# Input transfers of a fused three-layer kernel: fewer issued by ScalarE, full rows, and a work order planned anew

## The chip, the cores and the metric

The kernel runs on one core of a Trainium2 chip. The metric is the device time of one execution in microseconds (us). Engines: TensorE (PE, with PEld for its weight loads), VectorE (DVE), ScalarE (ACT), GpSimd (POOL) and SyncE (SP). DMA transfers are issued by SyncE or by ScalarE, each in the order of its own instructions ("SPq" and "ACTq" in the rows), and are carried out by 16 DMA engines.

## The reference

Three layers follow each other, for 4 batches of 576 tokens and 512 channels, all in 32-bit floats.

```python
# 1: attention, 8 heads of 64; 4 heads "local", 4 "strided"
mask_local   = (rel >= 0) & (rel < 32)
mask_strided = (rel >= 0) & (pos[None, :] % 32 == pos[:, None] % 32)
x = softmax(where(mask, q @ k.T / 8, -1e9)) @ v
# 2: feed-forward with the token before mixed in
xk = mu_k * x + (1 - mu_k) * x_prev ;  xr = mu_r * x + (1 - mu_r) * x_prev
x = sigmoid(xr @ w_r) * (relu(xk @ w_k) ** 2 @ w_v)      # w_r 512x512, w_k 512x1024, w_v 1024x512
# 3: four experts, each a causal attention of one head of 64; the two best by a gate are summed
out = sum over the token's two experts e of  weight_e * (softmax(q_e k_e.T / 8, causal) @ v_e @ wo_e)
```

The weights of layer 2 come as 64-bit floats, 10.5 MB in all.

## The kernel before

**Recording, planning, issuing.** The kernel does not call the engines in the order in which the work is written. A `Recorder` takes each operation as an `Op`, with what it needs, which buffers it opens and what it costs on each engine that could do it (`price`, L306). The operations are grouped in units with short names, and the string `PLAN` (L23) lists the names in an order that gives each operation its rank. `order` (L389) then plays the program through: for every engine it keeps the time at which it is free, finds the operations whose needs are met, and of those that could start within 0.1 us of the earliest takes the one of lowest rank. An operation whose buffer isn't free isn't a candidate (`begin`, L419). Operations that several engines can do (copies out of PSUM, casts) get their engine here. Where TensorE would stand idle in the first 80 us of that play, products on a tile of zeros are put in to keep it busy (`warm`, L378). The program is then issued in the planned order (`give`, L492 in every row), and each engine runs its own instructions in that order. So a changed cost or a changed string moves instructions everywhere, and no operation is added or lost by it but those warm-up products.

**How the planner times a transfer before.** A transfer issued by SyncE or ScalarE costs the issuer 0.45 us. Before the ninth issue *of one engine* it waits for the landing of that engine's eighth last (L423). The transfer then runs at 0.42 MB per us in the first 8 us and at 0.37 later, on one link, after 1.25 or 2.0 us (L465 to L468), and is counted as landed 0.5 us after that.

**Stage 1 of batch 0** is the head of the program. `pair(hp)` handles two heads: hp 0 and 1 are local, hp 2 and 3 strided. One tile `qkv` of a pair holds queries, keys and values, side by side; there are two such buffers for the local heads, and hp 2 and 3 of batch 0 live in buffers that other tiles use later. Its loads are the units `0L{hp}q` (`load`, L766), `0L{hp}v` (`load_rest`, L810) and `0L{hp}m` (`load_more`, L818). For the local pairs `q` brings the columns of the first two thirds of the tokens, `v` the values of those, `m` the rest; queries are issued by SyncE and keys, values, the local mask and the strided masks by ScalarE. `part` (L762) takes 96 rows (`LK`) for the columns of local values, which have content in 96 of 128 rows, and 128 for everything else. `0S` units hold the scores and the softmax of a third (local) or a group (strided), `0T` the transposes, `0V` the product with the values (tile `pol` or `pos`) that ends in `xT`. A softmax step is: scores on TensorE (`sl`, `ss`), minimum with the mask on VectorE, exponential on ScalarE (`el`, `es`), sum, reciprocal and product on VectorE. The transposes use the tile `ident`, loaded by unit `0i` (L1293).

**Weights.** `weight_pieces` (L620 and on) loads 20 pieces of 512 KB as tile `wraw`: 0 to 3 are w_r, 4 to 7 and 8 to 11 the two halves of w_k, 12 to 19 w_v. Unit `0L{j}` with a plain number is the load, `0W{j}` turns a piece into 32-bit floats (one ScalarE and two VectorE operations), `0P{j}` splits it into a high and a low part. All of them are issued by SyncE.

**Stage 2.** `0Ar`, `0Ak` mix the tokens of the first chunk (320 tokens), `0Ag` are its gate products with w_r (tile `pr`), `0Am` and `0Av` its products with w_k and w_v (tiles `pk`, `pv`); `0Z` are the same for the second chunk (256 tokens). Batches 1 to 3 follow with `1`, `2`, `3` in place of the leading 0; a load of a local pair of a later batch (`1L0`) is nine issues. Stage 3 has small letters.

The lines that order the loads of one local pair in batch 0, before:

```python
w, two = src.shape[1], nc.scalar
z = c + 6 * 2 * D if local else w

def part(a, z, q=nc.sync):
    rows = LK if local and a >= c else P
    q.dma_start(home()[:rows, a:z], src[:rows, a:z])
```

Of the kernel before, what the change touches and what calls it, by code (L numbers as in the profile page):

```python
# [22 lines left out]
PLAN = """  # L23
0L1q 0z 0L0q 0S3 1L1 0L1 wl3 1L0 0S0 0i 0T3 0L2q 0L2v 0L1v 0L3q 0S4 0T4 0V4 0L0v 0T0 0V0 0L3v 0S1 0S6 0L0m 0W1 0T1 0V1 0L15
0V3 0Ar0 0S7 0L0 0W0 0L1m 0L8 1z 0Ak0 0L3 0Ar1 0T7 0L11 0T6 0S9 0L2 0S8 0L6 0S2 0L13 0W2 0V7 0L7 0W7 0S5 0W3 ws30 0V6 0Ar2
0Ak2 0Ak1 0T9 0V9 0T8 0L12 0V8 0L4 0Ar3 0W6 0T5 wl0 ws00 0L5 0W5 0W4 0Ak3 0T2 0V2 0Zr0 0L10 0W10 0V5 0Zr1 0L18 0W18 1L2 0Ag0
0Ag1 0Zr2 0Zr3 0L14 0L9 0W13 1L3 0W9 2L2 0W11 0Am2 0Am3 0L17 0L16 ws31 0W8 0Zk0 ws01 0Am0 0W15 0W14 2L0 0Am1 0P5 2z 0Zk3 0P14
0Ag2 0Zg1 0L19 0W19 1S1 0W12 1S0 0Am4 0Am6 0Am7 0P18 0P6 wl2 2L1 0P19 0P13 0P12 0P15 0Zg3 0Zg0 0Av6 0W16 0P16 0Age 0P4 0Am5
0W17 0Av4 0Av0 0P17 0Zg2 0sig 0Av1 0Zk1 0P1 0P0 2L3 1S3 1S4 0Av5 0P8 1V1 1V4 0Av2 3L0 1S6 1T6 1S8 0Zk2 1V6 1Ar0 1Ak0 1Ar1
0Av3 1Zr0 3L1 1Ar2 1Ak1 0P3 0P7 0Zm2 0Zm3 0Zm0 0P10 3L2 0Av7 0x0 0P11 0P9 0Zm1 0Zm4 1Ak2 0u 0Zm5 0Zm6 0Zm7 0Zv4 0P2 1T8 0Zv6  # L30
0Zv2 0Zv0 1V8 1Ar3 1Ak3 0Zv1 1Am6 0Zv3 2S6 2T6 2V6 1Ag2 2S1 wl1 ws20 2S0 1Am4 2S4 2S3 1Ag0 2V1 2S8 1Ag3 1Zr2 1Ag1 3z 0Zv5
1Am5 1Zr1 1Am7 3L3 1Zr3 1Zg1 1Zg0 1Zk0 1Zk1 1Am2 1Am3 2V4 1Am0 1Am1 2T8 1Zk2 1Zk3 1Zm6 2Ar0 2Ar1 1Zm2 1Av0 0Zv7 1Zg2 2V8 2Ar3
1Zm7 1Zg3 1Av1 1Av4 1Av5 3S1 1Av2 3S0 1Av3 2Ar2 2Ag2 2Ag1 3V1 3S3 1Av6 1Av7 2Ag3 2Ak0 2Ak1 3S4 3V4 1Zm3 2Ag0 1Zm0 1Zm1 1Zv6
1Zm4 1Zm5 1Zv4 1Zv0 2Ak3 2Ak2 2Am0 2Am1 2Am2 2Am3 2Zr0 1Zv2 2Am6 2Am4 2Av4 2Zr1 2Zr2 2Am5 2Zk0 2Am7 1Zv3 1Zv1 2Zr3 1Zv5 2Zg2
2Zk1 2Zg0 3S6 2Zk2 2Zg1 ws10 2Zk3 2Zm4 2Av0 1Zv7 3Ar0 3Ar1 3Ak0 3Zr0 1u 0x1 2Zg3 2Av1 3T6 2Zm2 3V6 2Av6 2Av7 2Av2 2Zm3 2Zm0
2Zm6 2Zm5 3Ar2 3S8 3T8 3V8 1x0 2Zm1 2Zm7 2Zv0 2Zv2 2Zv3 2Zv4 2Zv5 2Av5 3Ar3 3Ag2 3Ak1 3Ak2 2Zv6 3Ag3 ws11 3Ak3 3Am0 3Am2 3Am3
3Zr1 2Zv1 3Am4 2Av3 3Ag1 3Am6 3Zr2 ws21 0v1 3Ag0 3Am5 3Am7 3Am1 3Zr3 3Zg0 3Zg2 3Zk0 3Zg1 3Av2 3Zk2 2Zv7 3Zg3 3Av6 3Av4 2u
3Zk1 3Zk3 3Zm4 3Zm0 3Av0 3Zm1 3Zm2 3Zm3 1x1 3Zm6 3Zm7 3Zm5 mc 3Av1 3Zv4 3u 3Zv0 3Zv6 3Zv2 0v0 0k00 0k01 0q01 0q00 0k10 0v4
0v2 0s0 0k11 1q01 0v3 0g 0m0 0s1 0m1 0p13 1q00 1v1 0q11 0q10 2x0 1k00 0s3 1n 1k01 1v2 0p02 3Av7 0p11 0p01 0s2 0p10 3Zv5 0p03
0t 0p00 0m2 0p22 0m3 0p32 0s40 0s41 0p23 1q10 1q11 1k10 1s1 0p20 0p21 1k11 1v0 0p33 0p12 1s2 0m4 0p41 0p30 0p31 3Zv7 1v3 1g  # L40
1m1 2q00 2k01 0p40 3Av5 1s3 1m3 1p31 0a10 0a11 0a00 0a01 1s0 2k00 0o02 1p32 1m2 3Zv1 0o01 3Zv3 2x1 2q10 1p21 0o03 2k10 1m0
1p12 1p03 1p02 1p10 1p11 1p01 2v2 0o12 1t 0o13 1s40 1s41 2v4 1p20 3n 1m4 3Av3 1p30 2q11 1p22 2t 0o00 2v1 1p41 2q01 0o10 1p23
1p00 2v0 2k11 2s1 1p13 2s40 0o11 1p40 3x0 3q00 2v3 2g 2m1 1p33 2s3 2m3 1a10 1a11 3x1 1a00 1a01 2s2 2m2 1o00 3k01 2p12 2p30
3q10 2p32 2s41 3k10 3q11 3k00 2p22 2p33 2p23 2s0 2m0 2p00 1o12 2m4 3v3 2p40 3v2 2p21 2p20 2p31 2p01 1o01 1o13 2p10 3k11 2p03
2p13 3v0 3v1 2p02 3g 2p11 3t 3s2 3s40 1o03 1o02 3s3 3q01 1o10 3s41 2p41 1o11 3s1 2a00 3m4 2a10 3m2 3p23 2a01 3m3 2a11 3s0
2o13 3p21 3m1 3p22 3p32 3p33 2o00 3p41 3p30 3p40 3m0 3p20 2o11 3p01 3p00 3p11 2o02 3p10 2o03 2o10 3p13 3p02 3p12 3p03 2o01
2o12 3a00 3a01 3p31 3a10 3a11 3o01 3o03 3o13 3o00 3o12 3o11 3o10 3o02
"""
# [1709 lines left out]
```

## Time and profile before

| | us |
|---|---|
| median of 3 runs (lowest, highest) | 509.03 (508.84, 509.15) |
| the profiled execution, its own time | 508.54 |
| its span, first to last instruction | 506.8 |
| TensorE busy in the span | 493.3 |
| VectorE busy | 348.4 |
| ScalarE busy | 280.1 |
| GpSimd busy | 8.6 |

The profile describes one execution. Its span is 1.74 us shorter than the time of the execution. Times in rows count from the span's start. "Busy" is the time in which an engine had an instruction in work; the queues' issuing instructions and waits are not counted. In a timeline a row can hold several like instructions that follow each other, and a wait stands in brackets with what ended it. The DMA share is the mean busy share of the 16 DMA engines.

### The profile page before, as it was taken

The numbers are of one execution on the slowest core, as the hardware profiler recorded it, in microseconds if no ns is written. First come the engines' busy times: TensorE is split into PE (matmuls) and PEld (weight loads), VectorE is DVE, ScalarE is ACT, GpSimd is POOL, SyncE is SP. The second block draws the span as 40 slices with busy tenths as digits, with TensorE's granted clock in tenths as the row PEclk, the third lists the DMA queues.
The fourth block names the chain that finished last, engine by engine and source line by source line (L and its number), as shares of the span: only waits on it lengthen the run. The fifth ranks groups of instructions, "written<-read, shape, count | busy, mean of one in ns | idle before, by whom it ended". The sixth has DMA issues, their size and how long they took to land.

```text
span 506.8 us, 13028 instructions
## 1 busy us (share of the span) xinstructions
PE 493.3 (97%) x5134; PEld 461.2 (91%) x5134; DVE 348.4 (69%) x1206; ACT 280.1 (55%) x831; POOL 8.6 (2%) x43
## 2 busy tenths in 40 slices
PE   4899999999999999999999999999999999999997
PEld 4767789999999999999999999999997998899896
DVE  1699999977858458553596813257999747886950
ACT  1799985646647355344534543124665654466663
POOL 0000000000000000000000000020000000000000
PEclk9599999999999999999999999999999999999999
DMA  8997211423423122000223300042103112001022
GB/s 267 343 396 245 69 63 58 154 61 101 105 69 85 46 83 85 32 1 23 73 64 96 103 27 27 22 117 58 43 1 95 32 38 78 18 27 34 27 95 93
DMA packets 34635, 43.79 MB, mean 86 GB/s; under 512 B 12790, under 2 KB 29006, under 8 KB 34574
## 3 DMA queue, kind: packets, MB, share of 16 engines
q1 hardware_dynamic: 33226, 41.38, 25.9%
q10 hardware_dynamic: 1348, 1.59, 1.0%
q8 instruction: 40, 0.66, 0.5%
q14 instruction: 21, 0.17, 0.1%
HBM read 33.38 MB, written 9.44 MB: 84 GB/s over the span
## 4 chain that ended last, share of the span: by engine, by line
PE 91%; DVE 4%; DMA 2%; ACT 2%; issue 0%; ACTq 0%
PE pk L492 21%; PE pv L492 20%; PE pr L492 10%; PE pvv L492 5%; PE pw L492 5%; PE pq_False L492 5%; PE pq_True L492 5%; PE pt L492 4%; PE s L492 4%; PE py L492 3%; PE ss L492 2%; PE pol L492 2%; PE sl L492 1%; PE ptl L492 1%; PE pos L492 1%; DMA qkv<-in_loc_dram 1%
## 5 line engine op out<-in xcount | busy, mean ns | idle before, releaser
L492 PE MATMUL pv<-kk,wvh 128*128 128x320 f32 (+1 forms) x512 | 103.1, 295 | 0.0
L492 PEld LDWEIGHTS pv<-kk,wvh 128*128 128x128 f32 x512 | 81.5, 188 | 0.5
L492 PE MATMUL pk<-xh,wkh 128*128 128x256 f32 (+1 forms) x224 | 65.7, 293 | 0.0
L492 PE MATMUL pk<-xl,wkh 128*128 128x256 f32 (+1 forms) x224 | 65.4, 292 | 0.0
L492 ACT ACTIVATE rf<-pk 128x320 f32<-128x320 f32 (+1 forms) x64 | 26.2, 410 | 45.0 <-PE pk L492 43.7
L492 ACT ACTIVATE pe<-pe,nm 128x128 f32<-128x128 f32 (+4 forms) x72 | 41.4, 577 | 9.0 <-DVE nm L492 4.7
L492 PEld LDWEIGHTS pk<-xh,wkh 128*128 128x128 f32 x224 | 42.0, 188 | 0.2
L492 PEld LDWEIGHTS pk<-xl,wkh 128*128 128x128 f32 x224 | 42.0, 188 | 0.0
L492 DVE TENSOR_TENSOR sg<-pv,sg 128x320 f32<-128x320 f32 (+1 forms) x32 | 14.6, 455 | 30.2 <-PE pv L492 20.9
L492 DVE CUSTOM_DVE_ANT_0 pe<-s,mcau 128x128 f32<-128x128 f32 (+4 forms) x72 | 32.1, 481 | 0.3 <-PE s L492 0.2
L492 DVE CAST kk<-rf 128x256 fp32r<-128x256 f32 (+1 forms) x41 | 12.6, 307 | 26.9 <-ACT rf L492 18.3
L492 DVE TENSOR_TENSOR kk<-rf,kk 128x320 fp32r<-128x320 f32 (+1 forms) x64 | 28.5, 454 | 2.3 <-ACT kk L492 1.5
L492 PE MATMUL pt<-ident,pe 128*128 128x128 f32 x200 | 30.0, 274 | 0.1
L492 ACT ACTIVATE rf<-rf 128x320 f32<-128x320 f32 (+1 forms) x64 | 28.5, 447 | 1.4
L492 PE MATMUL pr<-xh,wrh 128*128 128x320 f32 (+1 forms) x96 | 28.3, 295 | 0.0
L492 PE MATMUL pr<-xl,wrh 128*128 128x320 f32 (+1 forms) x96 | 28.2, 294 | 0.0
L492 DVE TENSOR_SCALAR pe<-pe,sm 128x384 f32<-128x384 f32 (+4 forms) x72 | 26.0, 400 | 0.2
L492 ACT COPY sg<-pr 128x320 f32<-128x320 f32 (+1 forms) x29 | 11.3, 406 | 26.5 <-PE pr L492 26.5
L492 DVE SCALAR_TENSOR_TENSOR xf<-xd,mu,xT 128x256 f32<-128x256 f32 (+1 forms) x52 | 25.5, 511 | 0.2
L492 ACT COPY aT<-pt 128x512 f32<-128x512 f32 (+3 forms) x52 | 22.5, 454 | 5.5 <-PE pt L492 4.9
L492 ACT ACTIVATE el<-el,nm 128x64 f32<-128x64 f32 (+1 forms) x72 | 24.8, 349 | 0.9 <-DVE nm L492 0.9
L492 PEld LDWEIGHTS pt<-ident,pe 128*128 128x128 f32 x200 | 23.3, 140 | 1.8 <-DVE pe L492 0.6
(309 smaller groups left out, 1445.0 us busy)
## 6 DMA issues: line engine op xcount, KB each, us to landing
wraw<-in_w_v_dram SPq DMA_DIRECT2D x8, 512.0 KB
wraw<-in_w_k_dram SPq DMA_DIRECT2D x8, 512.0 KB
qkv<-in_strd_dram SPq DMA_DIRECT2D x7, 576.0 KB
qkv<-in_loc_dram SPq DMA_DIRECT2D x6, 592.0 KB
x_spill<-sg SPq DMA_DIRECT2D x16, 160.0 KB
...
```

Of the source, the lines that this page charges most:

```text
L492: f[o.engine](*[now(x) for x in a], **{n: now(x) for n, x in k.items()})
```

## The change

It has four parts.

1. ScalarE issues only four transfers: the keys of `0L0q` (two) and `0L1q` (one), and the local mask. The identity (`0i`), the keys of the first strided pair, the values of both local pairs (`0L0v`, `0L1v`) and the two strided masks are issued by SyncE. The keys and queries of the first strided pair become one transfer.
2. Local values are loaded in all 128 rows instead of 96.
3. The planner's model of a transfer is another: its length follows from rows and contiguous runs, with a factor of 1.6 below 126 rows; the wait for the eighth last transfer counts the transfers of both queues together.
4. `PLAN` is another string, found with this model.

```diff
-0L1q 0z 0L0q 0S3 1L1 0L1 wl3 1L0 0S0 0i 0T3 0L2q 0L2v 0L1v 0L3q 0S4 0T4 0V4 0L0v 0T0 0V0 0L3v 0S1 0S6 0L0m 0W1 0T1 0V1 0L15
-0V3 0Ar0 0S7 0L0 0W0 0L1m 0L8 1z 0Ak0 0L3 0Ar1 0T7 0L11 0T6 0S9 0L2 0S8 0L6 0S2 0L13 0W2 0V7 0L7 0W7 0S5 0W3 ws30 0V6 0Ar2
...
+0L1q 0L0q 0S4 0S3 0i 0L3q 0T4 0T3 0L2q 0S1 0T1 0L1v 0S0 0z 0V3 0T0 0S6 1L0 0L1 0L0v 0V1 0V0 0L0m 0S7 0L1m 0S9 0Ar0 0W1 0T7 1u
+0L3 0W3 0V4 0Ar1 0T6 0L0 0W0 0S2 0Ak0 0L2v 0S8 0S5 0V7 0V6 0T9 0Ar2 0L3v 0V9 0L2 0W2 0L5 0L17 1z 0L6 0W6 0T2 0L7 0W5 0T8 0V8
...
@@ price
-            return 0.78 if v.p1 - v.p0 == 54 else 0.45, (v.p1 - v.p0) * v.cols.size * 4 / 1e6, None
+            rows, cols = v.p1 - v.p0, v.cols.reshape(-1)
+            run = int(np.argmax(np.append(np.diff(cols) != 1, True))) + 1
+            t = rows * cols.size / run / 16 * (run * 4 / 27500 + 0.0085) * (1.6 if rows < 126 else 1.0) + 0.07
+            return 0.78 if rows == 54 else 0.45, t, None
@@ order
-        ring = dict.fromkeys(self.ENGINES, 0.0)
-        mode, link, landed, given = None, 0.0, {e: [] for e in self.ENGINES}, []
+        mode, link, landed, given = None, 0.0, [], []
...
-            if o.load and e != "gpsimd" and len(landed[e]) >= 8:
-                s = max(s, landed[e][-8])
+            if o.load and e != "gpsimd" and len(landed) >= 8:
+                s = max(s, landed[-8])
...
-                t = max(ring[e], s + (1.25 if s < 8 else 2.0))
-                link = max(link, t) + o.lag[e] / (0.42 if s < 8 else 0.37)
-                ring[e] = max(link, t + (0.56 if s < 8 else 0.0))
-                o.end = ring[e] + 0.5
-                landed[e].append(o.end)
+                link = max(link, s + 1.5) + o.lag[e]
+                o.end = link + 0.8
+                landed.append(o.end)
@@ pair
             def part(a, z, q=nc.sync):
-                rows = LK if local and a >= c else P
-                q.dma_start(home()[:rows, a:z], src[:rows, a:z])
+                q.dma_start(home()[:, a:z], src[:, a:z])
...
-                    elif hp == 2:
-                        part(0, S)
-                        part(S, c, two)
...
-                    part(c, z, two if local else nc.sync)
+                    part(c, z)
                     if hp == 1:
                         for i, nr in enumerate((7, 6)):
-                            nc.scalar.dma_start(m0[nr], c_str[i, :NN * nr, :NN * nr])
+                            nc.sync.dma_start(m0[nr], c_str[i, :NN * nr, :NN * nr])
...
-    nc.unit("0i", lambda: nc.scalar.dma_start(ident, c_ident))
+    nc.unit("0i", lambda: nc.sync.dma_start(ident, c_ident))
```

## Rows read from the trace of the kernel before

**Rows 1.** The page's first part: busy time, share of the span and instructions by engine.

```profile
PE 493.3 (97%) x5134; PEld 461.2 (91%) x5134; DVE 348.4 (69%) x1206; ACT 280.1 (55%) x831; POOL 8.6 (2%) x43
```

**Rows 2.** Busy time by stretch, the first 30 us; columns in the first line.

```profile
core 0: us, PE busy (x) PEld busy (x) DVE busy (x) ACT busy (x) POOL busy (x), PEclk, DMA share, GB/s
0.00:10.00 10.00, 5.67 (x60) 5.09 (x60) 1.98 (x15) 0.00 (x0) 0.31 (x5) 1.00 0.81 256
10.00:20.00 10.00, 5.39 (x36) 4.74 (x34) 5.47 (x39) 8.05 (x34) 0.00 (x0) 0.53 1.06 317
20.00:30.00 10.00, 9.21 (x113) 7.30 (x112) 7.34 (x39) 7.52 (x34) 0.00 (x0) 0.78 1.03 391
```

**Rows 3.** The same view for the tile of zeros alone, the sum over 0 to 100.

```profile
sum 100.00, PE 4.84 PEld 4.33 DVE 0.17; mean PE 0.48 PEld 0.43 DVE 0.02
```

**Rows 4.** Timeline of ScalarE, 0 to 13.5 us: start, length, engine, instruction, count, [idle before].

```profile
0.73 0.89 ACTq L492 DMA_DIRECT2D qkv<-in_loc_dram  x2
1.65 0.45 ACTq L492 DMA_DIRECT2D mloc<-in_c_loc_dram  x1
2.13 0.45 ACTq L492 DMA_DIRECT2D qkv<-in_loc_dram  x1
3.94 0.33 ACTq L492 DMA_DIRECT2D ident<-in_c_ident_dram  x1
4.79 0.34 ACTq L492 DMA_DIRECT2D qkv<-in_strd_dram  x1
5.74 0.34 ACTq L492 DMA_DIRECT2D qkv<-in_loc_dram  x1
8.05 1.05 ACTq L492 DMA_DIRECT2D mstr<-in_c_str_dram  x2
10.83 0.32 ACTq L492 DMA_DIRECT2D qkv<-in_loc_dram  x1
11.18 1.28 ACT L492 ACT_TABLE_LOAD   x1 [11.18 <-DMA qkv<-in_loc_dram]
12.48 0.37 ACT L492 ACTIVATE el<-el,nm 128x96 f32<-128x96 f32 x1
```

**Rows 5.** Timeline of SyncE's queue, parts of 0 to 53 us.

```profile
0.73 1.33 SPq L492 DMA_DIRECT2D qkv<-in_loc_dram  x3
2.11 0.43 SPq L492 DMA_DIRECT2D wraw<-in_w_r_dram  x1
...
14.10 0.43 SPq L492 DMA_DIRECT2D wraw<-in_w_r_dram  x1
...
42.92 9.97 SPq L492 DMA_DIRECT2D qkv<-in_loc_dram  x17
```

**Rows 6.** Timeline of VectorE, parts of 5 to 14 us.

```profile
5.86 0.26 DVE L492 CUSTOM_DVE_ANT_0 el<-sl,mloc 128x96 f32<-128x96 f32 x1 [4.86 <-DMA mloc<-in_c_loc_dram]
...
13.69 0.17 DVE L492 TENSOR_SCALAR sm<-sm 128x3 f32<-128x3 f32 x1 [5.95 <-ACT el L492]
```

**Rows 7.** Timeline of TensorE, parts of 0 to 32.5 us.

```profile
14.74 0.84 PE L492 MATMUL ptl<-ident,el 128*96 128x128 f32 x3 [4.61 <-ACT el L492]
...
23.12 0.91 PE L492 MATMUL pol<-aTl,qkv 96*64 96x64 f32 x12
...
31.79 0.81 PE L492 MATMUL pr<-xw,w('r', 0)_378 128*128 128x320 f32 x2
```

**Rows 8.** Busy time by stretch, four others; columns as in rows 2.

```profile
12.48:31.79 19.31, 16.19 (x167) 13.35 (x167) 14.60 (x88) 16.08 (x73) 0.01 (x1) 0.69 1.04 367
31.79:100.00 68.21, 67.96 (x802) 56.63 (x803) 66.94 (x211) 57.16 (x169) 0.79 (x5) 1.00 0.44 142
450.00:506.80 56.80, 53.48 (x459) 47.59 (x457) 32.65 (x132) 32.97 (x97) 0.15 (x1) 0.99 0.18 61
...
14.00:16.00 2.00, 1.26 (x7) 0.93 (x9) 1.96 (x18) 2.00 (x11) 0.00 (x0) 0.50 1.10 268
```

**Rows 9.** Waits of SyncE's queue, 0 to 60 us: total, times, longest.

```profile
SPq L492 <- PE pol L492: 6.7, 1, 6.7
```

More of the change, by code (lines that the diff above doesn't have):

```diff
@@ L23 @@
 PLAN = """
-0L1q 0z 0L0q 0S3 1L1 0L1 wl3 1L0 0S0 0i 0T3 0L2q 0L2v 0L1v 0L3q 0S4 0T4 0V4 0L0v 0T0 0V0 0L3v 0S1 0S6 0L0m 0W1 0T1 0V1 0L15
-0V3 0Ar0 0S7 0L0 0W0 0L1m 0L8 1z 0Ak0 0L3 0Ar1 0T7 0L11 0T6 0S9 0L2 0S8 0L6 0S2 0L13 0W2 0V7 0L7 0W7 0S5 0W3 ws30 0V6 0Ar2
-0Ak2 0Ak1 0T9 0V9 0T8 0L12 0V8 0L4 0Ar3 0W6 0T5 wl0 ws00 0L5 0W5 0W4 0Ak3 0T2 0V2 0Zr0 0L10 0W10 0V5 0Zr1 0L18 0W18 1L2 0Ag0
-0Ag1 0Zr2 0Zr3 0L14 0L9 0W13 1L3 0W9 2L2 0W11 0Am2 0Am3 0L17 0L16 ws31 0W8 0Zk0 ws01 0Am0 0W15 0W14 2L0 0Am1 0P5 2z 0Zk3 0P14
@@ L28 @@
[L28 to L46, printed above, removed]
@@ L47 @@
-2o12 3a00 3a01 3p31 3a10 3a11 3o01 3o03 3o13 3o00 3o12 3o11 3o10 3o02
+0L1q 0L0q 0S4 0S3 0i 0L3q 0T4 0T3 0L2q 0S1 0T1 0L1v 0S0 0z 0V3 0T0 0S6 1L0 0L1 0L0v 0V1 0V0 0L0m 0S7 0L1m 0S9 0Ar0 0W1 0T7 1u
+0L3 0W3 0V4 0Ar1 0T6 0L0 0W0 0S2 0Ak0 0L2v 0S8 0S5 0V7 0V6 0T9 0Ar2 0L3v 0V9 0L2 0W2 0L5 0L17 1z 0L6 0W6 0T2 0L7 0W5 0T8 0V8
+0L4 1L1 0W4 0L13 0L8 0Ag0 0Ar3 0Ak3 0L16 0W7 0Ag1 0Ag2 0Ak1 0Ak2 0Am2 0T5 0L11 0Am0 0Am1 0W8 0L19 0W13 0Am3 0L15 0W15 0L18
+wl2 0P4 0V2 0Zr0 1L2 0Zr2 0Zr3 0V5 0Zr1 0Zg1 0L10 0W10 0L9 0W9 0W18 0Zg2 1L3 0L12 0Zk0 0L14 0W11 1S1 1S0 0W12 0P18 0P5 0Am6
@@ new lines @@
+0Am7 0W14 0P13 0P12 0P14 0P15 0W16 0W19 0P19 0P16 0W17 0P17 1V1 0Zg3 0Am4 0Am5 0P8 0P9 1S3 1S4 1V4 0Zk3 0Zg0 0Age 0sig 0Av0
+0Av2 0P1 0Av1 2z 1S6 1T6 0Av6 0Av4 0P7 0Av5 2L2 0Zk1 0Zk2 0P6 0Zm2 0P10 0Av3 0Av7 0x0 0P11 0Zm6 wl1 ws10 0P3 0P2 2L0 1V6 1S8
+1T8 1V8 0Zm3 2L3 0Zm4 0Zm5 wl0 2S6 3z ws11 2L1 0Zm0 0Zm1 1Ar0 1Ar2 0Zv0 1Ar1 0Zv2 0Zm7 1Ar3 0Zv6 1Ak0 1Ak3 2T6 0Zv7 0Zv1 1Ak1
+1Ak2 1Am2 1Am6 1Am3 1Zr0 2S1 1Zr1 0Zv4 0P0 1Ag0 2S0 1Ag1 1Ag2 0Zv5 ws21 2V1 2Ar0 0Zv3 1Zk0 1Ag3 1Am4 1Am0 1Am1 1Am5 1Am7 2u
@@ new lines @@
+3L1 1Av2 1Zr3 1Zr2 1Zg1 1Zg2 1Zg0 1Zg3 1Av0 1Av1 1Av4 1Zk2 2V6 2Ar2 3L0 1Av6 2S8 2T8 1Zk3 2V8 2S4 2S3 1Zk1 1Zm6 1Zm2 1Zm0
+1Zm1 1Zm3 1Zv2 1Zm4 1Zm5 1Zv0 1Zm7 2V4 2Ar3 2Ak0 2Ak2 2Ar1 2Ag0 1Zv3 1Zv4 3S3 1Zv6 1Zv7 2Ak1 2Ak3 1Zv1 1Av3 2Ag1 2Zr0 2Zk0
+2Zr2 1Zv5 3S4 2Am0 2Zr3 3S1 2Zk3 2Zk2 2Am6 wl3 2Am4 2Am5 2Am7 2Am2 1Av5 2Ag2 1Av7 3V4 3L2 2Am1 3S0 3V1 2Ag3 2Zr1 3Ar0 2Am3
+2Av0 2Zg2 2Zg0 2Zg1 2Av4 2Zg3 3L3 3S6 3T6 3V6 2Av5 2Av1 2Av6 2Av2 ws30 2Av7 2Zk1 3S8 3T8 2Zm6 2Zm2 3Ar1 2Zm4 2Zm0 2Zm1 2Zm7
+2Zm3 2Zm5 3Ar2 3Ak0 3Ak2 2Zv0 2Av3 2Zv6 3V8 3Ar3 2Zv1 2Zv2 2Zv7 3Ag2 3Ak3 3Ag1 3Ag0 3Ak1 3Am6 2Zv4 3Ag3 ws00 3Am0 3Am4 3Zr0
@@ new lines @@
+3Am1 0x1 3Am5 3Zk0 3Zr3 3Am7 3Am2 3Zr1 3Zr2 3Zk2 3Zk1 3Am3 2Zv3 3Zg1 ws20 2Zv5 3Zg2 0v1 3Zk3 3Zm0 3Zm1 3Zg0 3Zg3 3Av6 3Av0
+3Av2 3Av4 3Zm6 3Zm4 0u 3Zm2 3Zm3 3Zm7 3Zm5 3Zv2 3Zv4 3Zv6 3Zv0 0v0 0k00 ws01 0k01 0q01 0q00 0k11 3Av1 0v4 mc 0s1 0v3 0v2 0g
+0s0 0m1 3Zv5 0m0 0p11 3Av5 0p00 3Zv1 0p01 0k10 0q11 0p10 0q10 0p13 1x0 1v0 1q01 0p03 1k00 0s2 1x1 1k10 0p02 0s3 2x0 0m3 1v2
+0m2 0t 0p20 0p30 3Zv7 0p22 0s40 1q00 0s41 0p12 0m4 0p23 0p33 0p32 0p41 1v1 1n 3Zv3 1k01 2x1 1v3 0p21 0p31 0p40 1k11 1q10 2k01
@@ new lines @@
+1q11 3u 1s1 0a10 0a11 0a00 0a01 1s3 2k10 1g 1m1 1s0 1m3 1p12 1p13 1p31 1p10 2v1 ws31 0o13 0o03 1s2 1m0 1t 1p01 2v4 1p32 0o12
+1p02 2q10 2k00 0o10 1p03 3Av7 1m2 1p20 1s40 2k11 2q11 2t 0o11 2q01 1p22 1s41 1m4 1p41 1p30 2v2 3Av3 3x1 2s3 2v3 1p23 1p33 2v0
+2g 2q00 2s40 3q11 1p21 1p40 0o00 1p00 3k10 3k11 3q10 2s41 1p11 0o02 0o01 2s2 1a10 1a11 1a00 1a01 2m2 2s1 3x0 3k00 2m1 2p12
+3v3 2m4 2m3 2s0 3t 3q00 2p30 2p40 2p20 1o10 2p13 1o03 2m0 2p32 2p33 2p00 3k01 2p22 1o13 3v1 3s2 3v2 1o02 2p23 3v0 2p02 2p01
@@ L48 @@
+1o01 2p10 2p41 3q01 2p03 3n 2p21 3s40 3s41 2p11 1o12 1o00 3s1 3g 3m2 3m4 1o11 3s3 3m3 3p23 2p31 2a10 2a11 3p33 3p21 3p22 2a00
+2a01 3m1 3p30 3p40 3s0 3m0 2o01 3p32 3p41 3p01 3p00 2o13 3p13 3p02 3p03 3p11 2o10 2o12 2o03 2o02 2o11 3p10 3p12 2o00 3a00
+3a01 3p31 3p20 3a10 3a11 3o03 3o00 3o10 3o02 3o13 3o12 3o11 3o01
 """
```

## The prediction

> **What bounds the kernel now.** I read the page first, then the head of the run by stretches, then each engine's timeline there. The page has TensorE busy for 97% of the span [rows 1], so only what it does besides work can be won. The stretches say where that is: of the first 30 us it is busy 5.67, 5.39 and 9.21 us [rows 2], so 9.73 us idle, and 4.84 us of its busy time is warm-up products on the tile of zeros [rows 3]. That makes 14.6 us without work in the first 30, besides granted clocks of 0.53 and 0.78 in two of the stretches, that is, a good part of them at the lower level of 1.2 GHz. From 31.79 us to 100 us it is busy 67.96 of 68.21 us, and the last 56.8 us hold 3.32 us of idleness [rows 8]. What can be gained lies at the head.
>
> ScalarE's timeline [rows 4] says why the head is long. Its first four issues end at 2.58 us. The fifth, the identity, starts at 3.94 only, and then each issue starts late: 4.79, 5.74, 8.05, 10.83. None of them needs data. Eight issues, four on each queue, were started by 2.13 us without a wait [rows 4, 5]; from the ninth on each waits until the one eight places before it has landed, whichever queue issued that. So ScalarE stands in its own issues until 11.15 us; the table load follows at 11.18 and the first exponential at 12.48. VectorE shows what this costs [rows 6]: the mask lands and it takes the first row maximum at 5.86, and from 7.74 it stands for 5.95 us, to 13.69, until ScalarE's exponentials. TensorE waits 4.61 us for the same tile and transposes at 14.74, has its first product with values at 23.12 and its first gate product at 31.79 [rows 7]. After that it doesn't stop.
>
> **The change part by part.** *Issues taken off ScalarE.* Six go: the identity, the keys of the first strided pair, both local value blocks and the two strided masks. What is left are the four that now start between 0.73 and 2.13 us; they are among the first eight in the new order too (the first two tokens that load ask for seven transfers, four of them ScalarE's), so none should wait. If the identity came between, the fourth would be the ninth and start at about 3.94, which still costs nothing, since ScalarE's first input is there at 5.86. ScalarE is then free at 2.58, the table load of 1.28 us ends at 3.9, long before that input, and the first exponential can start when the first maximum is read, at about 6.1 instead of 12.48: **6.4 us earlier**. VectorE gets back its wait of 5.95 us. From 12.48 to 31.79 ScalarE is busy 16.08 of 19.31 us and VectorE 14.60 [rows 8]: this stretch is ScalarE's, and moves as a whole. From 31.79 to 100 VectorE is the fuller one, 66.94 of 68.21 us, so TensorE can start its products early and go on only if VectorE is early too. I take the smaller of both shifts, 5.95, as **6.0 us**.
>
> *Issues put on SyncE.* The six took 0.33, 0.34, 0.34, 1.05 (two) and 0.32 us, 2.38 us in all; the strided keys are merged with the queries into one transfer of 576 KB, so SyncE issues five more. Behind them in SyncE's queue stand the weight pieces. Each issue waits for a landing in any case, so what counts is the place in the common order, not the queue. Piece 0 of the gate weights was issued at 14.10 [rows 5] and first multiplied at 31.79. The flight of a transfer with seven others beside it is read off ScalarE: issued at 2.13 and waited for at 8.05, 5.9 us; issued at 4.79 and waited for at 10.83, 6.0 us. 17.7 us less 6.0 of flight and 6.0 of shift leaves a cover of 5.7 us, and the new order puts the four gate pieces ahead of those of the other weights, where before pieces of both others stood between. 2.4 us of issuing fit. Taken at 0; without the cover, 2.4 us lost.
>
> *Local values in 128 rows.* Two transfers of 96 rows by 3,072 bytes and two of 96 by 1,536, 885 KB together, become 1,180 KB. No row prices a 128-row one alone. From above: the 295 KB more at the 367 GB/s of the head [rows 8] are 0.80 us, all of it on the path. From below: if the 268 GB/s of 14 to 16 us, when such transfers were under way, are due to the 96 rows, then 885 KB took 3.30 us, and 1,180 KB at 367 GB/s take 3.21: a gain of 0.1 us. I take 0, because the values are first used at 23.12, 17 us after their issue at 5.74. The Trainium skill, "DMA: Bandwidth & Descriptors", section "Why a DMA increments its semaphore by 16 and not by 1", has a transfer of 96 partitions on all 16 engines just like one of 128; by it the extra rows are bytes and nothing else, and the sum would stand 0.8 us higher. The rate of the one stretch leans the other way, but smaller transfers ran in it as well.
>
> *The planned order and its costs.* Plan and costs are used before the program is issued; what they bring is another order on each engine. In the head it is planned with the wait that the trace shows. For the rest I take 0: the middle has no idleness to win, and the end's 3.32 us bound it from both sides. Half of that, 1.7 us, either way goes into the range.
>
> **The sum.** The profiled execution took 508.54 us (span 506.8 and 1.74 around it); less 6.0 this gives 502.5. The median of the runs shown, 509.03, is 0.49 above that execution, so **503.0 us**.
>
> **The rivals.** *More than the shift.* ScalarE still idles 19.31 - 16.08 = 3.2 us in its stretch, part of it while TensorE ran at half its clock. If no pause cools TensorE now and the order packs better, that comes too: 6.4 + 3.2 = 9.6 us, 499.4. Against it: the DMA engines' share is 1.04 there [rows 8], so data would have to come earlier than they can.
>
> *Only the issue time is won.* If the head is really set by the arrival of data (share about 1.0 from the second stretch of 10 us on), ScalarE's early start turns into waits for qkv and weights, and only the 2.38 us of issues are gained: 506.6. For it speaks that share; against it, that the gate weights lay ready long before use and that VectorE and TensorE name ScalarE, not a transfer, as what they waited for. In the Trainium skill, same page, section "Issuing engines are not separate DMA queues", issuing from several engines saves the initiating time alone; by that rule this is all that can change hands. The held issues from 3.94 to 10.83 show a cost that the rule doesn't have.
>
> *Slower: SyncE blocks.* With nearly every load on one queue, a transfer whose buffer is not free holds all behind it. Before, SyncE waited 6.7 us for the values' product to free the first qkv buffer, and then spent 9.97 us on 17 issues of the next batch's local heads, from 42.92 [rows 5, 9]. The new plan names such a load ahead of most weights. If it got there with its buffer not free, it would delay the weights by 16.7 us, against a cover of 5.7: 11 us late, 5.0 net, 514.0. It decides only if that load is issued ahead of the last gate weights, before about 20 us. Against it: the planner starts no load whose buffer is taken, and these buffers come free only when the third part of the local heads is through.
>
> *No change.* The new order of the middle or the end gives the gain of the head back: 509.0. Nothing in the profile speaks for it except that 5,134 products are ordered anew.
>
> **How the numbers follow.** A difference under 0.2%, 1.0 us, can't be told from none here. Forecast (501.0 to 505.5) 0.57; more than the shift 0.10; only the issue time (505.5 to 508.0) 0.17; no change 0.06; slower 0.10. Faster is the sum of the first three, 0.84. The range goes from 499.4, the whole of the larger case, to 508.0, the edge of what counts as faster; beyond it lie the 0.16 of no change and slower and a few hundredths below.
>
> **What would show it.** Right: no issue on ScalarE after about 3 us, the table load before 5 us and the first exponential near 6.1; VectorE's wait of 5.95 us gone; the first gate product near 25.5 instead of 31.79; TensorE's idle and warm-up time in the first 30 us down from 14.6 to about 8.6; and the middle as dense as before. Wrong: ScalarE's exponentials waiting for a qkv transfer or a mask; gate products waiting for weights whose issue on SyncE moved behind the next batch's loads; a first gate product near 25.5 but gaps on TensorE between 40 and 100 us, where VectorE would be the one that didn't follow; or an end with more than 3.3 us of idleness.

## The result, and the profile after

The changed kernel took 501.92 us (median of 4 runs, 501.2 to 502.88), the kernel before 508.93 beside it (508.7 to 509.15). The ratio is 0.9863, interval [0.9846, 0.9881], so 7.0 us faster, between 6.1 and 7.8. The profiled execution took 501.2 us. Its page, first the span, then busy time by engine:

```profile
span 499.4 us, 13036 instructions
...
PE 490.8 (98%) x5134; PEld 458.5 (92%) x5134; DVE 348.7 (70%) x1206; ACT 283.2 (57%) x831; POOL 7.9 (2%) x43
```

The stretches that answer to [rows 2] and [rows 8], and one from the middle (columns as there):

```profile
0.00:10.00 10.00, 7.64 (x68) 6.94 (x69) 3.34 (x28) 4.59 (x18) 0.31 (x5) 1.00 0.78 258
10.00:20.00 10.00, 8.78 (x132) 6.82 (x131) 9.71 (x68) 9.83 (x46) 0.00 (x0) 1.00 1.05 362
20.00:30.00 10.00, 9.19 (x67) 6.74 (x68) 9.85 (x48) 10.00 (x38) 0.26 (x2) 1.00 1.02 411
...
31.79:100.00 68.21, 68.13 (x906) 58.88 (x903) 65.40 (x187) 54.57 (x155) 0.51 (x3) 1.00 0.46 145
...
100.00:120.00 20.00, 19.02 (x214) 18.72 (x213) 15.23 (x56) 9.23 (x34) 0.20 (x1) 1.00 0.18 48
...
450.00:499.40 49.40, 46.22 (x400) 40.44 (x398) 28.02 (x113) 28.95 (x83) 0.00 (x0) 1.00 0.19 64
```

And the tile of zeros alone, as in [rows 3]:

```profile
sum 100.00, PE 4.96 PEld 4.27 DVE 0.17; mean PE 0.50 PEld 0.43 DVE 0.02
```

TensorE is idle for 2.36 + 1.22 + 0.81 = 4.4 us of the first 30, and 5.0 us are warm-up: 9.4 us without work instead of 14.6. VectorE and ScalarE are now nearly full from 10 us on. The granted clock, 0.53 and 0.78 in two of these stretches before, is 1.00 from 10 us on: TensorE doesn't fall back from its higher level, 2.4 GHz, any more.

The clock's column misleads at the start, here and in [rows 2]. The trace's record of the clock begins at 8.31 us, before the change at 7.27, and a time without a record is shown as 1.00. Up to there TensorE is as slow as in a stretch of 0.50. The products on zeros, all of one shape, show it. In the changed kernel four of them take 1.11 us before 8.31 and 0.66 behind it:

```profile
6.44 1.11 PE L492 MATMUL sl<-zeros 128*128 128x64 f32 x4
...
9.00 0.66 PE L492 MATMUL ptl<-zeros 128*128 128x64 f32 x4
```

In the kernel before, ten take 1.33 us at the higher level, and twelve 2.82 us in the part of [rows 2] that shows 0.53:

```profile
8.80 1.33 PE L492 MATMUL ptl<-zeros 128*128 128x64 f32 x10
...
17.74 2.82 PE L492 MATMUL ptl<-zeros 128*128 128x64 f32 x12
```

From one to the next it is 213 ns in the slow rows and 112 in the fast ones.

So TensorE is at its lower level, 1.2 GHz, up to 8.3 us in the changed kernel, and up to 7.3 and again from 10.7 to 24.3 us in the kernel before. Two things changed in the head of these two profiles, and the forecast had credited one.

ScalarE's timeline (compare [rows 4]):

```profile
0.73 0.89 ACTq L492 DMA_DIRECT2D qkv<-in_loc_dram  x2
1.65 0.45 ACTq L492 DMA_DIRECT2D mloc<-in_c_loc_dram  x1
2.13 0.45 ACTq L492 DMA_DIRECT2D qkv<-in_loc_dram  x1
2.62 1.28 ACT L492 ACT_TABLE_LOAD   x1 [2.62 <-issue]
5.91 0.38 ACT L492 ACTIVATE el<-el,nm 128x96 f32<-128x96 f32 x1 [2.00 <-DVE nm L492]
```

VectorE's first row maximum, which that exponential waits for (compare [rows 6]; no wait of 5.95 us follows any more):

```profile
5.61 0.26 DVE L492 CUSTOM_DVE_ANT_0 el<-sl,mloc 128x96 f32<-128x96 f32 x1 [4.61 <-PE sl L492]
```

TensorE (compare [rows 7]): first transposes, first product with values, first gate product, and one wait far behind the head:

```profile
9.61 0.50 PE L492 MATMUL ptl<-ident,el 128*96 128x128 f32 x3
...
12.26 0.57 PE L492 MATMUL pol<-aTl,qkv 96*64 96x64 f32 x12
...
25.16 0.81 PE L492 MATMUL pr<-xw,w('r', 0)_457 128*128 128x320 f32 x2
...
102.90 1.21 PE L492 MATMUL sl<-qkv 64*32 64x64 f32 x72 [0.98 <-DMA qkv<-in_loc_dram]
```

SyncE's queue (compare [rows 5]):

```profile
2.11 0.43 SPq L492 DMA_DIRECT2D ident<-in_c_ident_dram  x1
...
7.05 0.42 SPq L492 DMA_DIRECT2D wraw<-in_w_r_dram  x1
7.52 5.04 SPq L492 DMA_DIRECT2D qkv<-in_loc_dram  x7
13.07 1.40 SPq L492 DMA_DIRECT2D wraw<-in_w_r_dram  x2
14.52 1.30 SPq L492 DMA_DIRECT2D qkv<-in_strd_dram  x2
15.86 0.44 SPq L492 DMA_DIRECT2D wraw<-in_w_r_dram  x1
```

The first exponential comes 6.57 us earlier and the first gate product 6.63, as forecast. Between them lies more than a shift: the first product with values comes 10.9 us earlier. SyncE's queue shows another sequence of loads. The identity and the local heads come first; the first gate piece moved from 2.11 to 7.05, and the strided pairs' values, which went out among the issues at 4.18 and 7.82 before, to 14.52, while the last gate piece went out at 15.86 instead of 18.88.

To compare whole heads I count TensorE's work: each product at the median interval that its kind takes in the kernel before, warm-up left out. 20 us of such work are done at 42.8 us before and at 34.4 after: a lead of 8.4 us. It is an estimate, from one profile of each kernel. The span gained 7.4, so about 1 us was given back later, and the wait at 102.90 is of that size: the third batch's local heads land late, in a place where before had TensorE busy throughout (20.00 of the 20 us from 100 to 120).

The traces also tell what a held issue waits for. In all kernels here the loads of both queues signal eight semaphores in turn, and from the ninth load on each issuing instruction waits for the semaphore that it will use again. So the hold is a wait that stands in the program's own instructions; no run here shows a limit of the DMA engines behind it.

### The profile page after: what moved, and what is told of

Same layout as the page of the kernel before. It is cut to its first block, busy times and chain, and to the rows that moved or that the text cites. A ratio compares the mean times of both kernels' runs of the same rounds, so it can differ in the third digit from the quotient of the medians.

```text
span 499.4 us, 13036 instructions
## 1 busy us (share of the span) xinstructions
PE 490.8 (98%) x5134; PEld 458.5 (92%) x5134; DVE 348.7 (70%) x1206; ACT 283.2 (57%) x831; POOL 7.9 (2%) x43
## 4 chain that ended last, share of the span: by engine, by line
PE 92%; ACT 3%; DMA 2%; DVE 2%; issue 0%; ACTq 0%; SPq 0%
PE pk L492 21%; PE pv L492 20%; PE pr L492 10%; PE pvv L492 5%; PE pq_True L492 5%; PE pw L492 5%; PE pq_False L492 5%; PE s L492 5%; PE py L492 4%; PE pt L492 4%; PE sl L492 2%; DMA qkv<-in_loc_dram 2%; PE pol L492 2%; PE ss L492 1%; ACT wraw L492 1%; PE pos L492 1%
## 5 line engine op out<-in xcount | busy, mean ns | idle before, releaser
L492 ACT ACTIVATE pe<-pe,nm 128x256 f32<-128x256 f32 (+4 forms) x72 | 41.6, 579 | 21.3 <-DVE nm L492 17.4
L492 DVE CAST kk<-rf 128x320 fp32r<-128x320 f32 (+1 forms) x45 | 13.9, 310 | 28.2 <-ACT rf L492 25.9
L492 DVE CUSTOM_DVE_ANT_0 pe<-s,mcau 128x384 f32<-128x384 f32 (+4 forms) x72 | 31.7, 482 | 1.8 <-PE s L492 1.2
L492 ACT ACTIVATE rf<-rf 128x320 f32<-128x320 f32 (+1 forms) x64 | 28.5, 445 | 1.5
L492 ACT COPY aT<-pt 128x512 f32<-128x512 f32 (+3 forms) x57 | 24.7, 461 | 5.1 <-PE pt L492 4.7
L492 DVE TENSOR_SCALAR pe<-pe,sm 128x256 f32<-128x256 f32 (+4 forms) x72 | 25.7, 397 | 0.3
```

The lines of the kernel that those rows point to most:

```text
L492: f[o.engine](*[now(x) for x in a], **{n: now(x) for n, x in k.items()})
```

## The experiments

The table gives for all kernels the ratio to the kernel before and, from the one profiled execution, its time, the start of the first transposes and of the first gate product, the stretches of the head in which TensorE is at 1.2 GHz, and the lead as above. The first such stretch ends where the record of the clock begins; up to there the products are as slow as shown above.

| | ratio [interval] | profiled | transposes | gate | at 1.2 GHz | lead |
|---|---|---|---|---|---|---|
| before | | 508.54 | 14.74 | 31.79 | to 7.3, 10.7 to 24.3 | 0 |
| after | 0.9863 [0.9846, 0.9881] | 501.2 | 9.61 | 25.16 | to 8.3 | 8.4 |
| e1 | 0.9938 [0.9913, 0.9963] | 506.95 | 9.64 | 30.52 | to 7.9, 14.7 to 31.8 | 1.2 |
| e2 | 0.9970 [0.9945, 0.9995] | 507.4 | 11.95 | 30.62 | to 18.3, 25.1 to 28.5 | 3.0 |
| e3 | 1.0246 [1.0215, 1.0276] | 522.13 | 11.65 | 43.48 | to 20.2, 23.7 to 47.5 | -13.1 |
| e4 | 0.9858 [0.9831, 0.9886] | 500.08 | 10.33 | 25.72 | to 10.8 | 7.9 |
| e5 | 0.9952 [0.9926, 0.9978] | 505.2 | 9.49 | 27.65 | to 7.0, 24.1 to 30.9 | 3.1 |
| e6 | 0.9845 [0.9810, 0.9881] | 501.07 | 8.57 | 24.13 | to 8.6 | 9.3 |
| e7 | 1.0046 [1.0015, 1.0078] | 510.95 | 19.11 | 33.61 | to 22.7 | -1.8 |
| e8 | 0.9979 [0.9948, 1.0009] | 509.46 | 9.94 | 30.00 | to 9.0, 15.9 to 29.5 | 0.8 |
| e9 | 0.9961 [0.9935, 0.9986] | 507.77 | 11.00 | 26.86 | to 15.9 | 3.3 |
| e10 | 0.9954 [0.9927, 0.9981] | 506.42 | 8.81 | 25.43 | to 7.4, 17.6 to 27.9 | 3.6 |
| e11 | 0.9990 [0.9972, 1.0009] | 507.48 | 11.07 | 29.65 | to 14.5 | 2.2 |
| e12 | 0.9944 [0.9919, 0.9969] | 506.0 | 10.42 | 27.13 | to 13.9 | 6.4 |

The course of the clock is not set by the kernel alone: of the 77 executions of the kernel before that were taken beside the experiments, the mean granted clock lies between 0.977 and 1.000. Nor do TensorE's own products set it. In the changed kernel, e4 and e12 TensorE does the same products up to there, at times within 0.2 us, and rises at 8.3, 10.8 and 13.9 us. e12 also shows what this is worth: TensorE's order in its head is that of the changed kernel, it is at 1.2 GHz for 5.6 us longer, and its gate product comes 2.0 us later. So a difference of 1 or 2 us between the heads of two single profiles can be the clock alone; what is said of times below rests on the medians of all executions.

### e1: only the issues move

The kernel before, each engine's order of work kept; the six issues are emitted by SyncE. (`via` names the engine that the plan counts with, then the one that issues.)

```diff
-    nc.unit("0i", lambda: nc.scalar.dma_start(ident, c_ident))
+    nc.unit("0i", lambda: nc.via("scalar", "sync", ident, c_ident))
...
-                    part(c, z, two if local else nc.sync)
...
+                        nc.via("scalar", "sync", home()[:LK, c:z], src[:LK, c:z])
```

> The kernel before, every engine's planned order kept; only the six issues go out on SyncE at the same places of the common order. Theory (the hold): ScalarE is free at 2.6 us, its first exponential comes near 6.1 us and the first gate product near 26, 502.5 to 504.5 us. Rival (the new order): the old order was planned for other landing times, so most of the gain needs the new plan, 506.5 to 509 us.

504.73 us, 3.2 us faster by the ratio (1.9 to 4.4): about half of the change's gain, and between the ranges of theory and rival. The profiled execution took 506.95, the longest of seven. Its head, in ScalarE's and TensorE's timelines:

```profile
5.88 0.38 ACT L495 ACTIVATE el<-el,nm 128x96 f32<-128x96 f32 x1 [1.98 <-DVE nm L495]
...
14.97 1.49 PE L495 MATMUL ptl<-ident,el 128*96 128x128 f32 x6 [1.51 <-DVE sm L495]
...
30.52 1.41 PE L495 MATMUL pr<-xw,w('r', 0)_378 128*128 128x320 f32 x2
```

The stretches, and one wait of VectorE's (total, times, longest):

```profile
14.00:16.00 2.00, 1.03 (x5) 1.02 (x6) 1.82 (x14) 1.60 (x8) 0.00 (x0) 0.68 1.07 237
16.00:30.00 14.00, 13.56 (x126) 10.47 (x126) 10.01 (x51) 9.68 (x39) 0.00 (x0) 0.50 1.02 342
```

```profile
DVE es L495 <- DMA mstr<-in_c_str_dram: 2.3, 2, 2.0
```

ScalarE starts as early as in the changed kernel, and the first transposes too. But VectorE then waits for the strided masks, TensorE has 1 us of idleness from 14 to 16, falls to 1.2 GHz there, and is busy at that clock for 13.56 of the next 14 us. Of 5.1 us won at the transposes, 1.3 are left at the first gate product in this execution. By the median 3.2 us of the 7.0 arrive: the shift alone is not the change.

### e2: the issues go back

The changed kernel, each engine's order kept; identity, strided masks and both value blocks are emitted by ScalarE again (the identity thereby becomes the ninth transfer).

```diff
-    nc.unit("0i", lambda: nc.sync.dma_start(ident, c_ident))
+    nc.unit("0i", lambda: nc.via("sync", "scalar", ident, c_ident))
...
-                    part(c, z)
...
+                        nc.via("sync", "scalar", home()[:, c:z], src[:, c:z])
```

> The changed kernel, every engine's planned order kept; the identity, the two strided masks and the two local value blocks are issued by ScalarE again at the same places of the common order. Theory (the hold): each of them waits for its landing slot at 5 to 7.5 us in ScalarE's queue and holds the exponentials behind it, first exponential 6.5 to 8 us, 502.5 to 504.5 us. Rival (only the issue time counts): five issues of 0.4 us, 503.9 us with the first exponential still near 5.9. Rival (the new order alone): 501.5 to 502.4 us.

506.56 us, above all three ranges. ScalarE and TensorE:

```profile
7.05 1.30 ACTq L495 DMA_DIRECT2D mstr<-in_c_str_dram  x2
8.39 1.28 ACT L495 ACT_TABLE_LOAD   x1 [8.39 <-DMA ident<-in_c_ident_dram]
9.68 0.37 ACT L495 ACTIVATE el<-el,nm 128x96 f32<-128x96 f32 x1
```

```profile
30.62 0.81 PE L495 MATMUL pr<-xw,w('r', 0)_457 128*128 128x320 f32 x2
```

The first exponential moves back by 3.8 us and the first gate product by 5.5. By the ratios 0.9970 - 0.9863, 5.4 us are lost, at least 3.3 between the near ends of the intervals. The issues themselves last 0.34 + 0.33 + 1.30 + 0.36 = 2.3 us, so it is the hold with what follows from it, not the issuing, that costs: the new order is worth little while ScalarE stands in its queue. How much of the 5.4 us goes by way of the clock is not separated. In the profile 2.3 of the 5.5 us are there at the first transposes; the other 3.1 come between these and the gate product, where the same products run 9.7 us at 1.2 GHz and in the changed kernel none.

### e3 and e8: the plan without the issues, the issues without the string

e3 is the kernel before with the new string and model; ScalarE keeps its issues, local values 96 rows. e8 is the changed kernel with the old string and 96 rows, so the old string planned by the new model.

```diff
 e3:
-            if o.load and e != "gpsimd" and len(landed[e]) >= 8:
+            if o.load and e != "gpsimd" and len(landed) >= 8:
 e8, as e3 and:
-                    part(c, z, two if local else nc.sync)
+                    part(c, z)
```

> The kernel before with the new plan string and the new transfer model, but its six transfers still issued by ScalarE and 96 rows for local values. Theory (the hold): ScalarE is held in its queue again, first exponential after 8 us, 505 to 509 us. Rival (the new order): the planner knows of the waits and puts the issues where they don't hurt, 502 to 503.5 us.

> The old plan string with everything else of the change except the 128 rows: issues on SyncE, new transfer times, the wait counted over both queues. Theory (knowing the wait is enough to order the head): 502 to 504 us, clock kept. Rival (the new string matters too): 505 us or more.

e3: 520.1 us, 12.5 us slower by the ratio and far above its theory's range. Its order puts units of work ahead of issues on ScalarE; the second strided mask goes out at 21.3 us, and TensorE waits behind VectorE twice:

```profile
21.30 0.31 ACTq L492 DMA_DIRECT2D mstr<-in_c_str_dram  x1
```

```profile
23.96 1.23 PE L492 MATMUL sl<-qkv 64*64 64x96 f32 x12 [3.75 <-DVE nm L492]
...
29.00 1.21 PE L492 MATMUL ss<-qkv 64*126 64x126 f32 x8 [3.81 <-DVE nm L492]
```

e8: 508.35 us, not to be told from before. ScalarE's first exponential is at 5.81, so the whole of the forecast's shift is there, and in the profiled execution nothing of it arrives: TensorE waits 1.67 us until 15.77 and is at 1.2 GHz from 15.9 to 29.5 us, much as in e1. The twelve executions lie far apart, from 504.4 to 511.1, so of e8 no more is shown than that it is slower than the changed kernel. Neither half does it alone.

### e4: 96 rows again

The changed kernel, order kept, local values cut to 96 rows when emitted.

```diff
-                q.dma_start(home()[:, a:z], src[:, a:z])
+                if local and a >= c:
+                    nc.narrow(home()[:, a:z], src[:, a:z], LK)
```

> The changed kernel with its planned order kept, but local values of batch 0 moved in 96 rows. Theory (the rows are covered): no change that can be told, 501.4 to 502.4 us. Rival (rows are only bytes, 295 KB fewer on a full path): 501.1 us. Rival (96 rows are slower than 128): 502.5 to 503.5 us.

500.47 us, below all three ranges, but no difference to the changed kernel that the intervals would show. The last number of these stretches, GB/s, differs greatly. First e4:

```profile
12.00:14.00 2.00, 2.00 (x36) 1.63 (x35) 1.70 (x14) 2.00 (x11) 0.00 (x0) 1.00 1.08 255
14.00:16.00 2.00, 2.00 (x37) 1.65 (x35) 1.88 (x15) 1.99 (x11) 0.00 (x0) 1.00 1.10 268
```

then the changed kernel:

```profile
12.00:14.00 2.00, 2.00 (x39) 1.72 (x37) 1.93 (x14) 1.94 (x11) 0.00 (x0) 1.00 1.07 366
14.00:16.00 2.00, 1.75 (x31) 1.24 (x27) 1.88 (x14) 1.99 (x11) 0.00 (x0) 1.00 1.08 378
```

With the DMA engines equally busy, the stretches with 96 rows move 1.41 to 1.44 times less, more than the 1.33 times fewer bytes. Other transfers share these stretches: in the first the mix is much the same in both kernels, in the second the changed kernel has more of the weight pieces under way. In the first, packets of 3,072 bytes, the length of a row of the local values, take 182 ns on the mean with 96 rows and 125 with 128; those of 768 bytes, which other transfers move beside them, are slower too, 54 and 39. So by this rate the rows cost no transfer time, and the forecast's lower bound was the nearer one. By the Trainium skill, "DMA: Bandwidth & Descriptors", section "Why a DMA increments its semaphore by 16 and not by 1", both widths run on all 16 engines; this does not foresee the difference in rate.

### e5, e6, e7: the clock

e5 is e1 with six warm-up products ahead of the transposes that come late there; e6 the changed kernel without warm-up products; e7 the kernel before with 18 more products in its pause after 10 us.

```diff
 e5:
+        n += {"ptl0_1_1": 6}.get(t.kw["name"], 0) if t else 0
 e6:
-    WARM, FILL, IDLE = 80.0, 0.8, 0.35
+    WARM, FILL, IDLE = 0.0, 0.8, 0.35
 e7:
+        n += {"ptl0_1_0": 18}.get(t.kw["name"], 0) if t else 0
```

> The kernel of the first experiment (the order before, six issues on SyncE) with six more warm-up products ahead of the transposes at 13.5 us. Theory (the clock): there TensorE went to half its clock at 14.7 us for 17 us and was busy throughout, so it was the bound; kept warm, the first gate product comes before 28 us instead of 30.5 and the time is 501.5 to 503.5 us. Rival (late landings): masks and gate weights land later in that order, the clock is not the bound, 504 to 505.5 us.

> The changed kernel without its 16 warm-up products on zeros, nothing else changed in the order. Theory (the clock): the granted clock falls to half somewhere before 30 us and 3 us or more of the gain are lost, 504 to 508 us. Rival (the gain is ScalarE's early start alone): 501.5 to 502.5 us, whatever the clock does.

> The kernel before, with 18 more warm-up products in TensorE's pause from 10.1 to 14.7 us, so that the clock is kept. Rival (the clock alone is most of the gain): 504 to 506 us. Theory (ScalarE's hold is what bounds the head before): 507.5 to 509 us, first gate product 30.5 to 31.8 us.

e7: 510.99 us, above both ranges. The fill was too long, the transposes start at 19.11, 4.4 us late, and it did not do what it was meant to: TensorE was busy without a gap, at 1.2 GHz, until 22.71 us, where the record of the clock begins. Its products on zeros follow each other as slowly, 213 ns apart, as those of the kernel before at 0.50; the 1.00 of the second stretch here is again a time with hardly any record. First the kernel before, then e7:

```profile
10.68:24.34 13.66, 9.60 (x67) 8.36 (x68) 7.64 (x56) 9.92 (x43) 0.00 (x0) 0.50 1.04 333
```

```profile
10.68:24.34 13.66, 13.66 (x82) 13.10 (x81) 5.51 (x40) 8.11 (x35) 0.00 (x0) 1.00 1.04 305
```

```profile
9.25 10.07 PE L493 MATMUL ptl<-zeros 128*128 128x64 f32 x46
```

From the transposes to the first gate product it takes 14.5 us instead of 17.05, with 3.6 us of it at 1.2 GHz instead of 9.6. But ScalarE and VectorE had 4.4 us more to work ahead, so these 2.5 us are no price of the clock. The rival, that the clock alone is most of the gain, was not tested by e7.

e5: 506.26 us, above both ranges; its interval overlaps e1's, so in time nothing is shown. In its profile the clock holds until 24 us and the lead is 3.1 instead of 1.2, but TensorE now meets data that isn't there:

```profile
22.60 0.71 PE L496 MATMUL sl<-qkv 64*64 64x96 f32 x12 [2.25 <-DMA qkv<-in_loc_dram]
```

e6: 501.16 us, as the changed kernel; the theory is refuted. Without the warm-up products TensorE is busy for only 4.92 of the first 10 us, its clock rises at 8.6 us, as with them at 8.3, and it doesn't fall in the dense work that follows:

```profile
0.00:10.00 10.00, 4.92 (x54) 4.37 (x54) 4.23 (x36) 5.29 (x22) 0.31 (x5) 1.00 0.81 260
10.00:20.00 10.00, 8.52 (x129) 6.53 (x128) 9.71 (x64) 9.98 (x46) 0.00 (x0) 1.00 1.05 376
```

So in the changed kernel it isn't the warm-up that brings or keeps the clock.

### e9 to e12: what of the string

e9 is the changed kernel with the old string. In e10 and e11 the batch-0 loads stand at the front of the string: the old string with the loads in the new one's sequence, and the new string with those of the old one. e12 is the control, the new string with its own loads at the front.

```diff
 e9:
-0L1q 0L0q 0S4 0S3 0i 0L3q 0T4 0T3 0L2q 0S1 0T1 0L1v 0S0 0z ...
+0L1q 0z 0L0q 0S3 1L1 0L1 wl3 1L0 0S0 0i 0T3 0L2q 0L2v 0L1v ...
 e10:
+0L1q 0L0q 0i 0L3q 0L2q 0L1v 0L1 0L0v 0L0m 0L1m 0L3 0L0 0L2v 0L3v ...
...
+0L14 0z 0S3 1L1 wl3 1L0 0S0 0T3 0S4 0T4 0V4 0T0 0V0 0S1 ...
 e12:
+0L1q 0L0q 0i 0L3q 0L2q 0L1v 0L1 0L0v 0L0m 0L1m 0L3 0L0 0L2v 0L3v ...
...
+0L14 0S4 0S3 0T4 0T3 0S1 0T1 0S0 0z 0V3 0T0 0S6 1L0 0V1 ...
```

> Everything of the change except its string: issues on SyncE, local values in 128 rows, the new model, but the plan string of the kernel before. Theory, the string carries the second half of the gain: about 508, as e8 (508.35, the same with 96 rows), first exponential near 5.8, first gate product near 30. Rival, the 128 rows carry it (e4 showed their transfers to run at 366 to 378 GB/s instead of 255 to 268): at or below 505, first gate product before 28. Rival, the shift of ScalarE alone carries all of it and e8 was slow for its 96 rows: 502 to 503.

> As e9, but the batch-0 loads and the identity stand at the front of the old string, in the sequence that they have in the new one; the units of work keep the old string's sequence. Theory, it is the sequence of the loads (the second strided pair and the gate weights earlier, the values of the first pair and the other weights later): 502 to 504, first gate product before 27. Rival, it is the sequence of the units of work in the head (strided scores ahead of local ones): at or above 506.5, first gate product near 30.

> The complement of e10: the new string's units of work, the batch-0 loads at the front in the old string's sequence. Theory, the loads' sequence: at or above 506, first gate product near 30 or later. Rival, the units' sequence: 502 to 504. If the two need each other (work planned for data that come in another order), this one is the slowest of the three, over 508, and e10 gains nothing either.

> Control for e10 and e11: the new string with its own batch-0 loads moved to its front, sequence kept. The head's order on TensorE is then that of the changed kernel. Expected 501 to 503, first gate product near 25.2. If it comes out above 504, moving the loads to the front has a cost of its own, and e10 and e11 are to be read against this one.

Measured: 506.79, 506.38, 507.94 and 505.95 us. (The difference of the sequences was put badly in e10's expectation: the queue shows the identity and the local values earlier, the first gate piece and the strided values later.)

e9 has the change's issues, rows and model and stays 4.9 us above it by the medians, with intervals that don't touch. That the string carries a large part is shown. Of the rivals, the shift alone is refuted; the rows are not quite: e9's time, between the ranges of its theory and of this rival, doesn't differ from e8's by the intervals, but its head does, with no fall of the clock after 15.9 us and a gate product 3.1 us earlier.

e12 missed its expectation. Its head is that of the changed kernel, 2.0 us later by the later rise of the clock, lead 6.4. But later it loses more than the changed kernel does in the same place, and the clock falls there for 3.4 us:

```profile
100.00:120.00 20.00, 18.27 (x195) 17.95 (x195) 13.93 (x54) 8.00 (x30) 0.20 (x1) 0.91 0.15 39
```

```profile
101.82 1.45 PE L489 MATMUL sl<-qkv 64*32 64x64 f32 x72 [1.73 <-DMA qkv<-in_loc_dram]
```

So moving loads to the front costs about 4 us by the medians, of which 2.0 come with the later clock in this profile, and e10 and e11 can be read by their heads only (the old string with its own loads in front was not tried). e10 has the earliest rise of the clock (7.4) and the earliest transposes of the four (8.81) and then a pause with ScalarE full; the clock falls behind it. Its stretches and the wait in the pause:

```profile
14.00:16.00 2.00, 0.58 (x7) 0.28 (x3) 2.00 (x12) 2.00 (x9) 0.00 (x0) 1.00 1.08 389
16.00:18.00 2.00, 1.65 (x28) 1.42 (x30) 1.31 (x11) 1.26 (x6) 0.00 (x0) 0.91 1.02 335
18.00:20.00 2.00, 2.00 (x24) 1.60 (x21) 1.25 (x5) 1.95 (x11) 0.00 (x0) 0.50 0.90 337
20.00:28.00 8.00, 7.90 (x54) 5.43 (x53) 6.71 (x39) 6.42 (x28) 0.00 (x0) 0.51 1.02 406
```

```profile
16.21 0.57 PE L489 MATMUL pol<-aTl,qkv 96*64 96x64 f32 x12 [1.63 <-ACT es L489]
```

e11 keeps the clock once it has risen at 14.5, but has its transposes at 11.07 as e9, and its first gate product waits for piece 0 of w_r. That piece was issued at 13.75 us, no later than in e12, but VectorE converts it behind piece 3, which was issued at 17.38 (13.01 in e12):

```profile
29.65 0.81 PE L489 MATMUL pr<-xw,w('r', 0)_477 128*128 128x320 f32 x2 [0.72 <-DVE w('r', 0)_477 L489]
```

After 6 us of TensorE's work the two with the new sequence of loads lead by 9.3 (e10) and 7.0 (e12), the two with the old one by 5.0 each (e9, e11). After 20 us e10 is down to 3.6 and e12 still at 6.4. So with the same work the new sequence of loads is 2.0 (e12 against e11) and 4.3 us (e10 against e9) ahead early; the second figure holds a clock that rose 8.5 us earlier in e10 and loads that e9 doesn't have in front. That the new sequence of work is what keeps this lead, dense enough to leave no pause, fits e10 and e12 but is not shown: these are single profiles, and their clocks differ. Neither sequence alone comes to e12's lead. How the 4 us and more of the string split in time between the two stays open, as does what part of them is the clock's later rise (15.9 us in e9's profile for 8.3), and why fronted loads make the third batch's heads land later.

## Why the prediction was right in its sum and wrong in a step

The time, 501.92, lies in the range and 1.1 us under the 503.0. Most of the signs named for it came too; idle and warm-up time is 9.4 us instead of 8.6, and the last 49.4 us hold 3.18 us of idleness.

**Issues off ScalarE: right as an event, mis-sized as a term.** No issue after 2.58 us, table load at 2.62, first exponential at 5.91 for 6.1, VectorE's wait gone, first gate product at 25.16 for 25.5. But the step "this stretch is ScalarE's, and moves as a whole", worth 6.0, does not hold by itself: alone the same shift brought 3.2 us (e1), with the old string under the new model nothing measurable (e8), with 128 rows 2.0 (e9). Taking it away costs 5.4 (e2). The stretch is ScalarE's only while ScalarE is late. In e1's profile, with ScalarE early, strided masks that land late open a pause. In size the rival *only the issue time is won*, 2.4 us, is nearer to e1's 3.2 than the forecast's 6.0.

**The planned order: the step that failed.** It was taken at 0, because the middle has no idleness to win. The order's effect lies in the head: between e1 and the changed kernel, whose intervals don't touch, are 3.8 us, and e9 gives the same answer. The head's order was to be re-planned for a free ScalarE; "planned with the wait that the trace shows" was in the text, and no price was put on it.

**The clock: not credited, its part open.** *More than the shift* had its condition right, "no pause cools TensorE now and the order packs better", and the head indeed leads by 8.4. TensorE's time at 1.2 GHz in the head fell from 21 to 8.3 us in the two profiles. What this is worth of the 7.0 us no run shows: e12's 2.0 us for 5.6 us hold for a head in which TensorE was busy, and in the kernel before it stood idle for 4.1 of the 13.7 us after 10.7. The end didn't come to 499.4 since about 1 us went back at 102.90.

**SyncE's issues at 0: right.** Of the four gate pieces two were issued 4.1 and 3.0 us earlier and one 4.9 us later; piece 0, which is multiplied first, was issued at 14.14 us, as before, and used 11.0 us later. SyncE stands 5.04 us in seven issues and nobody waits for it. The rival *SyncE blocks* did not come: the 17 issues of the next local heads, 13.03 us long, start at 34.72, behind the gate weights. e11 shows how near it is: with a gate piece issued 4.4 us later, the first gate product waits 0.7 us for conversions.

**Rows at 0: right** in the changed kernel (e4), for the reason given: the values are covered. **The rule of "Issuing engines are not separate DMA queues"** (the Trainium skill, "DMA: Bandwidth & Descriptors") had issuing time as all that can change hands: 2.4 us. e1's 1.9 to 4.4 would allow it; e2's loss of at least 3.3 for 2.3 us of issues does not, nor does its first exponential, 3.8 us later.

So what the forecast booked as one shift of 6.0 was a smaller shift and two terms left out, and it came close by luck: these happened to be of the size of what the shift lacked.
